# Causal attention and relu-squared MLP: six pairs scaled after the product with v, and two word conversions that may run on GpSimd

## Chip, cores, metric

One core of a Trainium2 chip runs the whole program. The metric is the device time of one execution in microseconds, lower is better.

## What is computed

q, k and v are float32 of shape (4 batches, 12 heads, 448 rows, 64 columns); w_in (768 x 2048) and w_out (2048 x 768) come as float64 words.

```python
scores = scale * q @ k.T            # causal mask, scale = 1/sqrt(64)
attn = exp(scores - max)            # masked
attn = attn / (sum(attn) + 1e-9)
x = (attn @ v)                      # laid out as 1792 tokens x 768
out = relu(x @ w_in)**2 @ w_out
```

## The kernel before

The program is written as a list of operations with ranks and dependencies (`plan.op`). A list scheduler, `Plan.emit`, gives each operation a place: at each step it takes the ready operation that can start first (ties by rank), and of the engines allowed for it (its "ways") the one that would end it first, with a small penalty of 0.5 us for ScalarE and 1.0 us for VectorE in the first part. Tiles from shared pools are taken and given back in that order, PSUM's eight banks too (kinds mm, sc, pt, av and others, each with a cap). The result is one fixed order for each engine's queue and for SyncE's DMA queue. Within a queue nothing overtakes: an instruction that waits holds up all that stand behind it.

Attention works on 24 pairs of heads. The first 12 (batches 0 and 1) are computed at the start, with two sets of buffers used in turn (`even`, names beginning with a, and `odd`, b). For one pair:

- `load_qk`, `load_v` (L349, L361): DMAs on SyncE; the first two pairs' q on ScalarE's queue.
- `transposed` (L367): VectorE turns k and q.
- `softmax` (L386): the scores of seven chunks of queries of 64 rows x 2 heads, chunk c against (c+1)*64 keys. The two heads of a chunk fill 128 partitions.
- `exponential`: VectorE adds the mask and takes the maximum (L399); ScalarE takes the exponential and its sum (L403) into the tiles p and sm.
- `inverse` (L470, L471): VectorE adds 1e-9 to the seven sums and inverts them.
- `normalise` (L412 on GpSimd, or L414 on VectorE): p of each of the seven chunks is multiplied in place by its inverse sums.
- `transposed_p` (L426): TensorE turns p in 16 blocks of 128 x 128, and ScalarE (L311) or VectorE (L434) copies four blocks at a time from PSUM to the tile pt.
- `times_v` (L446): v times pt gives x, transposed, in PSUM: 128 partitions (head and column) x 448 queries.
- For the first 12 pairs x is split into a float32r high part (ScalarE L311 from PSUM) and a low part (VectorE L314, PSUM minus high), both into x_t.

A next pair on the same buffers may write p only after the transposes of the pair before have read it.

Beside it the weights are brought in by `piece`: for each group gr (four in all) six pieces of w_in (128 x 512) and eight of w_out (128 x 384). A piece's float64 words are loaded (L587, three raw buffers), ScalarE converts the high word and the low word (two L311, words<-words), VectorE shifts, adds and joins them (L595, L314, L598), and `split` makes the high part on GpSimd (L324) or ScalarE and the low part on VectorE (L314) or GpSimd (L318). `h_unit` (L634 to L636) multiplies x of a half of the tokens by w_in; its two PSUM banks of kind mm let two columns of work be under way at once. Only the first group's w_in pieces are needed while the first pairs run.

After the first 12 pairs TensorE works on the MLP of the first two batches, group by group, with the other 12 pairs of attention put in between, and then on the second half of the tokens.

Of the kernel before, what the change touches and what calls it, by code (L numbers as in the profile page):

```python
# [9 lines left out]
F32 = mybir.dt.float32  # L10
F32R = mybir.dt.float32r
I32 = mybir.dt.int32
U32 = mybir.dt.uint32
I64 = mybir.dt.int64
AF = mybir.ActivationFunctionType
ALU = mybir.AluOpType

PE, ACT, DVE, POOL, DMA, DMA2 = range(6)
# [147 lines left out]
def t_dve(n, fast=False):  # L166
    return n / 1920 + 0.15 if fast else n / 960 + 0.15


def t_pool(n, two=False):  # L170
    return n * 0.0021 + 0.21 if two else n / 1200 + 0.22
# [9 lines left out]
def t_dma(count, size):  # L181
    return count * (0.0084 + size * 0.0000488) / 16
# [3 lines left out]
def kernel(  # L186
# [17 lines left out]
    nc = tc.nc  # L204
    B, H, S, D = q.shape
    DM = out.shape[1]
    DFF = w_in.shape[1]
    P = 128
    QC = P // 2
    NQ = S // QC  # L210
# [15 lines left out]
    PLACE = {6: (0, 0), 5: (1, 0), 0: (1, 6 * QC), 4: (2, 0), 1: (2, 5 * QC), 3: (3, 0), 2: (3, 4 * QC)}  # L226
# [10 lines left out]
    PCW = max(GF * P, CH)  # L237
    NRAW, NZ, NB, NR = 3, 3, 1, 6
    HWAY, OWAY, GWAY = slice(None), slice(1, 2), slice(0, 1)
    TURNS, LEAD = (0, 3, 2, 1), 15  # L240
    CB = NP // 2
    CBW = CB * P

# [15 lines left out]
    psum = ctx.enter_context(tc.tile_pool(name="psum", bufs=1, space=bass.MemoryType.PSUM))  # L259
    plan = Plan()  # L260

    def tiles(nm, n, shape, dtype, pool=const):
        return [pool.tile(shape, dtype, name=f"{nm}{i}") for i in range(n)]

    early = ExitStack()
    pool = early.enter_context(tc.tile_pool(name="early", bufs=1, side="right"))
    ident = pool.tile([P, 3 * QC], F32, name="ident")
# [3 lines left out]
    x_t = tiles("x", NA, [P, 2, S], F32R)  # L271
# [21 lines left out]
        nc.gpsimd.memset(t[KLAST:, NK - 1], 0.0)  # L293
    plan.pool("v", v_t)
    plan.pool("mx", tiles("mx", 8, [P, 1], F32))
    plan.pool("ps", tiles("ps", 8, [P, 512], F32, psum), mm=2, sc=4, pt=2, av=1, st=5, os=7)

    make_identity(nc, ident[:, :P])
    nc.vector.tensor_copy(ident[:, P:], ident[:, :QC])
# [1 line left out]
    for i in range(2):  # L301
        m = mask[i * QC:(i + 1) * QC, S - QC:]
        nc.gpsimd.affine_select(
            out=m, in_=m, pattern=[[-1, QC]], base=0,
# [5 lines left out]
    def on_act(n, dst, src, psum=False, func=AF.Copy, more=0, **kw):  # L310
        return (ACT, t_act(n, psum, more), lambda: nc.scalar.activation(dst(), src(), func, **kw))  # L311
# [8 lines left out]
    def two_sources(*args):  # L320
        return [on_dve(*args, 0.03) + SHARED, on_pool(*args)]
# [5 lines left out]
    def split(rank, n, hi, lo, src, reads, key, after=(), drop=(), take=None, ways=slice(None)):  # L327

        plan.op(rank, [copy_on_pool(n, hi, src), on_act(n, hi, src)],
                reads, [(key, 0)], after, drop=drop, take=take)  # L330
        plan.op(rank, two_sources(n, lo, src, lambda: hi().bitcast(F32), ALU.subtract)[ways],
                list(reads) + [(key, 0)], [(key, 1)], after, drop=drop)
# [4 lines left out]
    def attention(s, n, at):  # L337

        b, hp = divmod(n, NP)
# [68 lines left out]
        def normalise(c, keys, at):  # L408
            def operands():
                return probabilities(c), probabilities(c), s.sm[:, c:c + 1]  # L410
            plan.op(at, [
                (POOL, 0.00083 * CW[c] + 0.3, lambda: nc.gpsimd.tensor_scalar(  # L412
                    *operands(), 1.0, op0=ALU.mult, op1=ALU.mult)),
                (DVE, t_dve(CW[c], True) + 0.5, lambda: nc.vector.tensor_scalar(  # L414
                    *operands(), None, op0=ALU.mult)) + SHARED,
            ], keys, [(nm, "p", c)])

        def transposed_p(i, at):

            ps = Hold("ps", "pt")  # L420
            blocks = TURNED[4 * i:4 * i + 4]

            def go():
                for n, (c, kc) in enumerate(blocks):
                    o = QC * (PLACE[c][0] & 1)
                    nc.tensor.transpose(  # L426
                        ps.t[:, n * P:(n + 1) * P],
                        s.p[:, POFF[c] + kc * P:POFF[c] + (kc + 1) * P], ident[:, o:o + P])
            plan.op(at, [(PE, 4 * 0.109, go)], [(nm, "p", c) for c, _ in blocks], [ps],
                    take=ps, clear=[(nm, "pt", i)], lag=spare(1.6))  # L430
            t = s.pt[:, 4 * i * P:4 * (i + 1) * P]
            plan.op(at, [
                on_act(512, lambda: t, lambda: ps.t, True),
                (DVE, t_dve(512) + 0.05, lambda: nc.vector.tensor_copy(t, ps.t)),  # L434
            ], [ps], [(nm, "pt", i)], drop=[ps])
# [35 lines left out]
            nc.vector.reciprocal(s.sm, s.sm)  # L471
        keys = [(nm, "sm", c) for c in range(NQ)]
        plan.op(at, [(DVE, 0.4, inverse) + SHARED], [], keys)
        for c in range(NQ):
            normalise(c, keys, at)
        at += 2
        av = Hold("ps", "av")
        for i in range(len(TURNED) // 4):
            transposed_p(i, at)
        times_v(av, at + 1)  # L480
        at += 3
        if n < NA:
            x = x_t[n]
            plan.op(at, [on_act(S, lambda: x[:, 0], lambda: av.t[:, :S], True)],
                    [av], [(("x", n), 0)])
            plan.op(at, [on_dve(S, lambda: x[:, 1], lambda: av.t[:, :S],
                                lambda: x[:, 0].bitcast(F32), ALU.subtract)],
                    [av, (("x", n), 0)], [(("x", n), 1)], drop=[av])
        else:
            spill(n - NA, av, at)  # L490
# [69 lines left out]
    def piece(rank, kind, gr, a, ch, after):  # L560
        mark = len(plan.ops)
        if kind == "i":
            src = w_in[a * P:(a + 1) * P, gr * GF * P:(gr + 1) * GF * P]
            key = ("wi", a)
        else:
            f = gr * GF + a
            src = w_out[f * P:(f + 1) * P, ch * CH:(ch + 1) * CH]
            key = ("wo", a, ch)
        n = src.shape[1]
        raw, zt, bt = Hold("raw", "raw"), Hold("z", "z"), Hold("b", "b")  # L570

        def word(i):
            return raw.t.bitcast(I32).rearrange("p (c t) -> p c t", t=2)[:, :n, i]

        def z():
            return zt.t[:, :n]

        def zf():
            return z().bitcast(F32)

        def b():
            return bt.t[:, :n]

        def dst(i):
            return wi_t[:, i, a] if kind == "i" else late["wo"][:, i, a, ch * CH:(ch + 1) * CH]

        plan.op(rank - 12, [(DMA, 0.5, lambda: nc.sync.dma_start(out=raw.t[:, :n], in_=src), t_dma(P, 8 * n))],  # L587
                [], [raw], take=raw)

        plan.op(rank - 4, [on_act(n, zf, lambda: word(1).bitcast(F32), func=AF.Abs, scale=2.0 ** -112)],  # L590
                [raw], [zt], take=zt)

        plan.op(rank - 4, [on_act(n, b, lambda: word(0).bitcast(U32), scale=2.0 ** -29)],
                [raw], [bt], take=bt)
        plan.op(rank - 2, [(DVE, t_dve(n, True), lambda: nc.vector.tensor_scalar(  # L595
            z(), z(), 3, None, op0=ALU.logical_shift_left)) + SHARED], [], [zt])
        plan.op(rank - 2, [on_dve(n, z, z, b, ALU.add, 0.03) + SHARED], [bt], [zt], drop=[bt])
        plan.op(rank - 2, [(DVE, t_dve(n) + 0.03, lambda: nc.vector.scalar_tensor_tensor(  # L598
            out=z(), in0=word(1), scalar=-2 ** 31, in1=z(),
            op0=ALU.bitwise_and, op1=ALU.bitwise_or)) + SHARED], [raw], [zt], drop=[raw])  # L600
        split(rank, n, lambda: dst(0), lambda: dst(1), zf, [zt], key, after, [zt])
        if kind == "o":
            plan.op(rank, [(DMA, 0.5, lambda: nc.sync.dma_start(out=wo_dram[gr, a + GF * ch], in_=zf()), t_dma(P, 4 * CH))],
                    [zt], [("wod", gr, a, ch)], drop=[zt])
            if (a % 2, ch) != (0, 1) or gr == TURNS[-1]:
                plan.op(rank + 12, [(DMA, 0.5, lambda: nc.sync.dma_start(
                    out=wh_dram[gr, a + GF * ch],
                    in_=late["wo"][:, :, a, ch * CH:(ch + 1) * CH].bitcast(F32)), t_dma(2 * P, 4 * CH))],
                    [(key, i) for i in range(2)], [("whd", gr, a, ch)])
        if kind == "i" and gr > 0:  # L610
            plan.op(rank, [(DMA, 0.6, lambda: nc.sync.dma_start(
                out=wz_dram[gr, :, a // CB, :, a % CB].rearrange("f p n -> p f n"),
                in_=zf().rearrange("p (f n) -> p f n", n=P)), t_dma(P * GF, 4 * P))],
                [zt], [("wzd", gr, a)], drop=[zt])
        pieces.extend(plan.ops[mark:])
# [417 lines left out]
    PAIR = 8.6  # L1033
    H_US, O_US = 3 * t_mm(S), 3 * t_mm(CH)
    stack, middle = ExitStack(), ExitStack()
    odd = Buffers("b", stack.enter_context(tc.tile_pool(name="b", bufs=1)))
    for n in range(NA):
        attention((even, odd)[n % 2], n, n * PAIR)
    start = NA * PAIR + 4
# [36 lines left out]
    rank, begin = start, 10.0  # L1076
# [81 lines left out]
```

## Time and profile before

| What | us |
|---|---|
| Time, median of 3 runs (lowest to highest) | 615.87 (615.43 to 618.31) |
| Profiled execution: its own time | 616.22 |
| Profiled execution: span from first to last instruction | 614.5 |
| TensorE busy in the span | 589.3 |
| VectorE, ScalarE, GpSimd busy | 436.9, 356.7, 352.5 |

What lies outside the span of the profiled execution is 1.72 us. TensorE is counted busy while any of its matmuls is under way, also when one waits inside a group, so a busy engine may still work slower than it could.

### The profile page before, as it was taken

What the parts mean: (1) busy time and instruction counts of PE and PEld (TensorE: products, weight loads), DVE (VectorE), ACT (ScalarE), POOL (GpSimd) and SP (SyncE); (2) the same over time, 40 slices, a digit from 0 to 9 for tenths busy, and PEclk for the clock granted to TensorE, in tenths of its full rate; (3) what the DMA queues carried; (4) which work ended last, traced back from release to release, by engine and by line L of the source; (5) the groups of instructions that cost most, each with busy time, mean ns of one, the idle gap of its engine ahead of it and who ended that gap; (6) DMA issues with size and microseconds to landing.
All of it is one profiled execution on the core that took longest, in us unless ns stands there. A gap on an engine that the chain in (4) does not pass through costs nothing.

```text
span 614.5 us, 11390 instructions
## 1 busy us (share of the span) xinstructions
PE 589.3 (96%) x3714; PEld 511.0 (83%) x3714; DVE 436.9 (71%) x957; ACT 356.7 (58%) x878; POOL 352.5 (57%) x460
## 2 busy tenths in 40 slices
PE   3888999999999999999999999999999999999996
PEld 1555677789988988988998889989989999998995
DVE  4888776366786689785787326679994896399474
ACT  3787998657677845678555552247665534661220
POOL 2556575475589746788644764325865674478110
PEclk9899999999999999999999999999999999999999
DMA  9788856597888999998997477877958837963546
GB/s 140 159 199 146 175 99 132 106 308 243 249 222 256 293 264 220 275 265 277 245 279 249 163 209 220 266 219 194 228 103 198 224 71 161 221 105 95 149 76 106
DMA packets 203148, 120.01 MB, mean 195 GB/s; under 512 B 138960, under 2 KB 191056, under 8 KB 203088
## 3 DMA queue, kind: packets, MB, share of 16 engines
q1 hardware_dynamic: 181328, 108.01, 64.4%
q0 software_dynamic: 6912, 9.44, 10.2%
q10 hardware_dynamic: 14848, 1.84, 2.0%
q8 instruction: 29, 0.48, 0.3%
q14 instruction: 31, 0.25, 0.1%
HBM read 80.71 MB, written 38.54 MB: 194 GB/s over the span
## 4 chain that ended last, share of the span: by engine, by line
PE 81%; DVE 8%; DMA 5%; ACT 3%; issue 1%; POOL 1%; SPq 1%; DVEq 0%; ACTq 0%; POOLq 0%
PE ps L1010 7%; PE ps L634 7%; PE ps L1012 6%; PE ps L1011 6%; PE ps L636 6%; PE ps L635 6%; PE ps L426 6%; PE ps L446 6%; PE ps L386 5%; PE ps L937 5%; PE ps L939 5%; PE ps L938 5%; PE ps L815 4%; PE ps L811 4%; PE ps L813 4%; DVE g L314 2%
## 5 line engine op out<-in xcount | busy, mean ns | idle before, releaser
L412 POOL TENSOR_SCALAR ap<-ap,asm 128x128 f32<-128x128 f32 (+6 forms) x122 | 72.7, 615 | 52.3 <-DVE asm L471 41.6
L311 ACT ACTIVATE words<-words 128x384 f32<-128x384 f32 (+3 forms) x135 | 77.3, 596 | 32.9 <-DVE words L314 9.7
L399 DVE CUSTOM_DVE_ANT_0 ps<-ps,mask 128x448 f32<-128x448 f32 (+6 forms) x168 | 68.7, 444 | 28.2 <-PE ps L386 22.8
L1010 PE MATMUL ps<-wo,g 128*128 128x384 f32 x224 | 77.0, 344 | 0.0
L634 PE MATMUL ps<-x,wi 128*128 128x448 f32 x192 | 75.0, 391 | 0.6 <-ACT x L311 0.6
L1012 PE MATMUL ps<-wo,g 128*128 128x384 f32 x224 | 75.1, 335 | 0.0
L1011 PE MATMUL ps<-wo,g 128*128 128x384 f32 x224 | 75.0, 335 | 0.0
L636 PE MATMUL ps<-x,wi 128*128 128x448 f32 x192 | 70.9, 369 | 0.4 <-DVE wi L314 0.4
L635 PE MATMUL ps<-x,wi 128*128 128x448 f32 x192 | 70.7, 368 | 0.2 <-DVE x L314 0.2
L403 ACT ACTIVATE ap<-ps,mx 128x448 f32<-128x448 f32 (+6 forms) x126 | 58.7, 482 | 13.5 <-DVE mx L399 12.5
L937 PE MATMUL ps<-g,wi 128*128 128x448 f32 x162 | 59.5, 367 | 1.0 <-DVE sb L314 0.9
L311 ACT ACTIVATE r<-ps 128x448 f32<-128x448 f32 x59 | 32.1, 545 | 48.3 <-PE ps L815 15.8
L938 PE MATMUL ps<-g,wi 128*128 128x448 f32 x162 | 59.3, 366 | 0.0
L318 POOL TENSOR_TENSOR wi<-words,wi 128x384 fp32r<-128x384 f32 (+1 forms) x45 | 56.3, 1263 | 5.1 <-ACT wi L311 2.4
L939 PE MATMUL ps<-g,wi 128*128 128x448 f32 x162 | 59.2, 366 | 0.0
L324 POOL TENSOR_SCALAR wi<-words 128x384 fp32r<-128x384 f32 (+1 forms) x40 | 26.8, 672 | 47.4 <-DVE words L598 14.4
L811 PE MATMUL ps<-x,wi 128*128 128x448 f32 x141 | 51.8, 368 | 0.0
L813 PE MATMUL ps<-x,wi 128*128 128x448 f32 x141 | 51.7, 367 | 0.0
L815 PE MATMUL ps<-x,wi 128*128 128x448 f32 x141 | 51.7, 366 | 0.0
L314 DVE CUSTOM_DVE_ANT_0 words<-words 128x768 uint16<-128x768 uint16 (+1 forms) x56 | 45.7, 816 | 5.3 <-ACT words L311 1.9
L311 ACT ACTIVATE apt<-ps 128x512 f32<-128x512 f32 x70 | 38.4, 602 | 17.4 <-PE ps L426 17.4
L595 DVE TENSOR_SCALAR words<-words 128x384 int32<-128x384 int32 (+1 forms) x56 | 29.1, 521 | 21.5 <-ACT words L311 21.1
(138 smaller groups left out, 1476.1 us busy)
## 6 DMA issues: line engine op xcount, KB each, us to landing
words<-in_moe_w_in_dram SPq DMA_DIRECT2D x24, 512.0 KB, 5.3
words<-in_moe_w_out_dram SPq DMA_DIRECT2D x32, 384.0 KB, 4.2
wo_split<-wo SPq DMA_DIRECT2D x26, 384.0 KB, 4.8
wi<-wo_split SPq DMA_DIRECT2D x24, 384.0 KB, 4.5
wo_whole<-words SPq DMA_DIRECT2D x32, 192.0 KB, 4.0
wi_split<-wi SPq DMA_DIRECT2D x24, 256.0 KB, 4.0
v<-in_v_dram SPq DMA_DIRECT2D x24, 192.0 KB, 4.2
wi_whole<-words SPq DMA_DIRECT2D x18, 256.0 KB, 4.3
```

What stands on the lines that cost most here:

```text
L311: return (ACT, t_act(n, psum, more), lambda: nc.scalar.activation(dst(), src(), func, **kw))
L634: nc.tensor.matmul(o, w[:, 0], x[:, 0], start=c == 0, stop=False)
L635: nc.tensor.matmul(o, w[:, 0], x[:, 1], start=False, stop=False)
L636: nc.tensor.matmul(o, w[:, 1], x[:, 0], start=False, stop=c == NP - 1)
L811: nc.tensor.matmul(o, w.t[:, 0, c], x[:, 0], start=begin and c == 0, stop=False, skip_group_check=True)
L813: nc.tensor.matmul(o, w.t[:, 0, c], x[:, 1], start=False, stop=False, skip_group_check=True)
L937: nc.tensor.matmul(o, w.t[:, 0, d], g.t[:, 0], start=start, stop=False, skip_group_check=True)
L938: nc.tensor.matmul(o, w.t[:, 0, d], g.t[:, 1], start=False, stop=False, skip_group_check=True)
L939: nc.tensor.matmul(o, w.t[:, 1, d], g.t[:, 0], start=False, stop=stop, skip_group_check=True)
L1010: nc.tensor.matmul(res(), g[:, 0], w[:, 0], start=f == 0, stop=False)
L1011: nc.tensor.matmul(res(), g[:, 0], w[:, 1], start=False, stop=False)
L1012: nc.tensor.matmul(res(), g[:, 1], w[:, 0], start=False, stop=f == GF - 1)
```

## The change

For the first six pairs (n below 6, batch 0) p is left as the exponentials. `spread` takes the place of `normalise`: the inverse sums are laid on a stacked identity (VectorE or GpSimd, 128 x 448 elements), seven float32 matmuls of 64 columns with a 128 x 128 matrix of ones and zeros (`heads`) bring each query's factor to all partitions of its head, and the result is copied from PSUM to a tile xs (ScalarE or VectorE). After `times_v`, VectorE multiplies x in PSUM by xs into xs, and `split` makes the high part (GpSimd or ScalarE) and the low part (VectorE or GpSimd) from it. For the first group's pieces (gr 0) both word conversions get GpSimd as a second way. Some constants are set up on GpSimd at the start, and PSUM gets one more kind, rb, with a cap of one.

```diff
+    LATER = 6
-    TURNS, LEAD = (0, 3, 2, 1), 15
+    TURNS, LEAD, WORDS = (0, 3, 2, 1), 15, 0
@@
-    plan.pool("ps", tiles("ps", 8, [P, 512], F32, psum), mm=2, sc=4, pt=2, av=1, st=5, os=7)
+    plan.pool("ps", tiles("ps", 8, [P, 512], F32, psum), mm=2, sc=4, pt=2, av=1, rb=1, st=5, os=7)
@@
+        def spread(keys, at):
+            i = n % 2
+            rb = scaled[i].rearrange("p (c i) -> p c i", i=QC)
+            ps = Hold("ps", "rb")
+            plan.op(at, two_sources(S, lambda: rb, lambda: stacked[:, None, :].to_broadcast([P, NQ, QC]),
+                                    lambda: s.sm[:, :, None].to_broadcast([P, NQ, QC]), ALU.mult), keys, [("scaled", i)])
+            def go():
+                for c in range(NQ):
+                    cols = slice(c * QC, (c + 1) * QC)
+                    nc.tensor.matmul(ps.t[:, cols], heads[PLACE[c][0] & 1], scaled[i][:, cols],
+                                     start=True, stop=True, skip_group_check=True)
+            plan.op(at, [(PE, 0.8, go)], [("scaled", i)], [ps], take=ps)
+            xs = Hold("r", "xs")
+            plan.op(at, [on_act(S, lambda: xs.t, lambda: ps.t[:, :S], True),
+                         (DVE, t_dve(S) + 0.05, lambda: nc.vector.tensor_copy(xs.t, ps.t[:, :S]))],
+                    [ps], [xs], take=xs, drop=[ps])
+            return xs
@@
-        for c in range(NQ):
-            normalise(c, keys, at)
+        late_scale = n < LATER
+        if late_scale:
+            factors = spread(keys, at + 1)
+        else:
+            for c in range(NQ):
+                normalise(c, keys, at)
@@
+        if late_scale:
+            x, xs = x_t[n], factors
+            plan.op(at, [(DVE, t_dve(S) + 0.05, lambda: nc.vector.tensor_tensor(
+                out=xs.t, in0=av.t[:, :S], in1=xs.t, op=ALU.mult))], [av], [xs], drop=[av])
+            split(at, S, lambda: x[:, 0], lambda: x[:, 1], lambda: xs.t, [xs], ("x", n), drop=[xs])
+            return
@@
+        def early_pool(dst, src, scale):
+            return [] if gr > WORDS else [(POOL, t_pool(n), lambda: nc.gpsimd.tensor_scalar(
+                dst(), src(), scale, 1.0, op0=ALU.mult, op1=ALU.mult))]
@@
-        plan.op(rank - 4, [on_act(n, zf, lambda: word(1).bitcast(F32), func=AF.Abs, scale=2.0 ** -112)],
+        plan.op(rank - 4, [on_act(n, zf, lambda: word(1).bitcast(F32), func=AF.Abs, scale=2.0 ** -112)] + early_pool(
+            zf, lambda: word(1).bitcast(F32), 2.0 ** -112),
@@
-        plan.op(rank - 4, [on_act(n, b, lambda: word(0).bitcast(U32), scale=2.0 ** -29)],
+        plan.op(rank - 4, [on_act(n, b, lambda: word(0).bitcast(U32), scale=2.0 ** -29)] + early_pool(
+            b, lambda: word(0).bitcast(U32), 2.0 ** -29),
@@
+    stacked, heads = pool.tile([P, QC], F32, name="stacked"), tiles("heads", 2, [P, P], F32, pool)
+    nc.gpsimd.tensor_tensor(out=stacked, in0=ident[:, :QC], in1=ident[:, QC:P], op=ALU.add)
+    for h in range(2):
+        nc.gpsimd.memset(heads[h], 0.0)
+        for j in range(2):
+            nc.gpsimd.memset(heads[h][(j ^ h) * QC:((j ^ h) + 1) * QC, j * QC:(j + 1) * QC], 1.0)
```

## Rows read from the trace of the kernel before

**Rows 1.** The page's part 1: busy us, share of the span, instructions
```profile
PE 589.3 (96%) x3714; PEld 511.0 (83%) x3714; DVE 436.9 (71%) x957; ACT 356.7 (58%) x878; POOL 352.5 (57%) x460
```

**Rows 2.** Busy time by stage: us, per engine (instructions), granted clock, DMA share, GB/s
```profile
core 0: us, PE busy (x) PEld busy (x) DVE busy (x) ACT busy (x) POOL busy (x), PEclk, DMA share, GB/s
7.00:20.00 13.00, 8.74 (x80) 5.67 (x82) 9.01 (x35) 7.79 (x28) 3.20 (x7) 1.00 0.94 168
20.00:60.00 40.00, 34.71 (x306) 22.76 (x296) 34.16 (x110) 30.95 (x93) 22.72 (x41) 0.96 0.82 168
60.00:66.00 6.00, 4.82 (x30) 3.92 (x30) 2.56 (x7) 5.64 (x19) 2.70 (x3) 0.72 0.99 212
66.00:73.00 7.00, 6.73 (x60) 4.76 (x62) 6.64 (x23) 6.42 (x23) 5.36 (x9) 1.00 0.79 164
73.00:117.00 44.00, 44.00 (x384) 32.65 (x378) 30.04 (x107) 36.44 (x111) 22.89 (x41) 1.00 0.52 98
```

**Rows 3.** TensorE's timeline, 0 to 75 us: start, us, what, count, [idle before <-releaser]
```profile
13.42 3.09 PE L386 MATMUL ps<-bkt,bqt 64*64 64x448 f32 x28 [3.23 <-DVE asm L470]
...
19.46 0.99 PE L386 MATMUL ps<-akt,aqt 64*64 64x448 f32 x12 [1.03 <-ACT bp L403]
...
24.15 1.52 PE L426 MATMUL ps<-ident,bp 128*128 128x128 f32 x4 [0.77 <-POOL bp L412]
...
30.37 1.75 PE L386 MATMUL ps<-bkt,bqt 64*64 64x448 f32 x28
...
36.41 0.66 PE L426 MATMUL ps<-ident,ap 128*128 128x128 f32 x4 [0.77 <-ACT apt L311]
...
45.49 2.80 PE L386 MATMUL ps<-bkt,bqt 64*64 64x448 f32 x28 [1.02 <-ACT bpt L311]
...
61.18 1.94 PE L426 MATMUL ps<-ident,bp 128*128 128x128 f32 x8 [2.55 <-ACT ap L403]
...
66.26 1.95 PE L446 MATMUL ps<-bpt,v 128*64 128x448 f32 x16
```

**Rows 4.** ScalarE's timeline, the same columns
```profile
32.20 1.27 ACT L311 ACTIVATE words<-words 128x512 f32<-128x512 f32 x2 [1.07 <-DMA words<-in_moe_w_in_dram]
...
44.28 0.68 ACT L311 ACTIVATE words<-words 128x512 f32<-128x512 f32 x1 [1.71 <-DMA words<-in_moe_w_in_dram]
...
59.20 1.22 ACT L311 ACTIVATE words<-words 128x512 f32<-128x512 f32 x2 [3.09 <-DMA words<-in_moe_w_in_dram]
```

**Rows 5.** Granted clock around the two slow places, columns as in Rows 2
```profile
26.00:28.00 2.00, 1.62 (x5) 1.38 (x5) 1.74 (x7) 1.98 (x9) 1.47 (x2) 0.61 0.67 110
28.00:30.00 2.00, 2.00 (x11) 1.88 (x10) 0.93 (x4) 0.60 (x1) 1.16 (x4) 0.54 0.66 121
...
60.00:62.00 2.00, 0.82 (x4) 0.78 (x5) 0.64 (x3) 2.00 (x8) 1.92 (x3) 0.64 0.92 110
62.00:64.00 2.00, 2.00 (x9) 1.81 (x8) 1.48 (x3) 2.00 (x5) 0.78 (x1) 0.50 0.83 312
```

**Rows 6.** GpSimd's timeline, 0 to 75 us
```profile
13.86 3.20 POOL L412 TENSOR_SCALAR ap<-ap,asm 128x64 f32<-128x64 f32 x7 [10.85 <-DVE asm L471]
...
45.16 1.27 POOL L318 TENSOR_TENSOR wi<-words,wi 128x512 fp32r<-128x512 f32 x1
...
55.27 4.32 POOL L412 TENSOR_SCALAR bp<-bp,bsm 128x64 f32<-128x64 f32 x7
```

**Rows 7.** Chain that ended last, in order of time: start, us, what
```profile
105.66 1.31 PE ps L426 x12
```

**Rows 8.** Groups by form, 0 to 70 us: busy us, mean ns
```profile
L314 DVE TENSOR_TENSOR x<-ps,x 128x448 fp32r<-128x448 f32 x6 | 3.7, 614 | 1.9 <-ACT x L311 1.9
...
L324 POOL TENSOR_SCALAR wi<-words 128x512 fp32r<-128x512 f32 x5 | 3.1, 617 | 14.9 <-DVE bsm L470 8.9 <-DVE words L598 6.1
```

**Rows 9.** VectorE's timeline, 0 to 75 us
```profile
34.32 0.14 DVE L399 DVE_READ_ACCUMULATOR2_ANT mx<- 128x1 f32 x1
...
45.38 1.33 DVE L595 TENSOR_SCALAR words<-words 128x512 int32<-128x512 int32 x1
```

More of the change, by code (lines that the diff above doesn't have):

```diff
@@ L1035 @@
     stack, middle = ExitStack(), ExitStack()
-    odd = Buffers("b", stack.enter_context(tc.tile_pool(name="b", bufs=1)))
+    pool = stack.enter_context(tc.tile_pool(name="b", bufs=1))
+    odd, scaled = Buffers("b", pool), tiles("scaled", 2, [P, S], F32, pool)
+    stacked, heads = pool.tile([P, QC], F32, name="stacked"), tiles("heads", 2, [P, P], F32, pool)
[4 more added lines that the diff above has]
+            nc.gpsimd.memset(heads[h][(j ^ h) * QC:((j ^ h) + 1) * QC, j * QC:(j + 1) * QC], 1.0)
     for n in range(NA):
```

## The prediction, on record before the change was timed

> **What bounds the kernel now.** I read the page's busy times first: TensorE is busy 589.3 of 614.5 us [rows 1]. A change to softmax can then win only where TensorE stands, or works below its pace, and it loses wherever it gives TensorE work that finds no gap. The second view, busy time by stage, says where the 25.2 us of idle time lie. From 7 to 73 us TensorE stands for 4.26 + 5.29 + 1.18 + 0.27 = 11.0 us; before 7 us it waits for the first loads; from 73 to 117 us it stands for nothing [rows 2]. So the six pairs that the change touches run in the one long stage in which TensorE is not the bound: the sixth pair's product with v starts at 66.26 us [rows 3]. If x of the sixth pair comes d us earlier, the full stretch behind it starts d earlier, and, since TensorE is the bound from there on, the end comes d earlier too.
>
> Which wait ends last in that stage is told by TensorE's timeline: 3.23 us before the second pair's scores and 1.03 before the third's, 0.77 us for normalised p, 0.77 and 1.02 us for ScalarE's copies out of PSUM, and 2.55 us at 58.6 us, the largest in the middle [rows 3]. The first two belong to the loading of q and k, which nothing here makes faster (the DMA engines are at 0.94 from 7 to 20 us [rows 2]). Behind the later ones ScalarE's timeline shows the same cause three times: its queue stood 1.07, 1.71 and 3.09 us at a conversion of weight words whose load had not landed [rows 4], and the copies and exponentials stood behind it. Last, the granted clock: it is at 0.61 and 0.54 from 26 to 30 us and at 0.64 and 0.50 from 60 to 64 us, each time after TensorE had worked little or stood, so there part of the work ran at 1.2 GHz [rows 5].
>
> No engine has much room: from 20 to 60 us VectorE is busy 34.16 of 40 us (85%), ScalarE 30.95 (77%), GpSimd 22.72 (57%), DMA at 0.82 [rows 2]. A gain there meets VectorE soon.
>
> **The change part by part.**
>
> Normalising goes. It is seven instructions a pair on GpSimd, 3.20 us when alone and 4.32 us when disturbed [rows 6], between the last exponential and the last transpose, and the next pair on the same buffers waits for those transposes. On TensorE's path this shows as 0.77 us at 24.15. The half clock from 26 to 30 us follows that slow stretch; TensorE is busy 1.62 + 2.00 us in those 4 us [rows 5], so some 1.7 us would be won with full clock there. Ends: 0.8 (the wait alone) and 2.5. I take 1.8, since most, but not all, of the idleness ahead of the clock's fall was that wait.
>
> Words may go to GpSimd. Two conversions for each of the six w_in pieces, 12 in all. No row shows GpSimd doing them; the nearest is its copy of 128 x 512 at 617 ns, and the far bound its two-source operation of that width at 1.27 us [rows 6, 8]. That is 7.4 to 15.2 us for GpSimd; I take 0.7 each, 8.4 us, against about 6 x 3.4 = 20 us of normalising that it loses. What matters is that a wait for a load then blocks GpSimd and not ScalarE. At 58.6 us TensorE gets back up to 2.55 us, and up to half of the 2.82 us that it worked at the low clock from 60 to 64, 1.4 us, so 0 to 3.95; I take 3.0, as the 3.09 us wait of ScalarE covers the whole of it [rows 3 to 5]. At 45.5 us it is 1.02 us of standing and the stretch of the scores there (2.80 us where the same 28 took 1.75 at 30.37 [rows 3]), so 0 to 2.07; I take 1.2. At 36.41 us, behind the 1.07 us wait, 0 to 0.77; I take 0.7, the shortest wait being most surely gone. The eight w_out pieces of the first group lie mostly after 73 us, where GpSimd and ScalarE have room (22.9 and 36.4 of 44 us [rows 2]): nothing; without that room 16 x 0.6 us of GpSimd.
>
> Queued behind a waiting conversion on GpSimd stand the stacked product, the high and low parts of x and the normalising of the seventh and later pairs; TensorE waits for each of them in turn, for the first at the seven new matmuls. That is the first rival.
>
> New matmuls. Seven float32 products of 64 columns with 128 x 128 weights for a pair; float32 products stand in this trace as two instructions each (28 for the 14 scores), so 14. The nearest rows are the transposes, with the same weights and 128 columns: 12 in 1.31 us, 109 ns each [rows 7]. So 14 x 0.109 = 1.5 us is the upper end, and half, 0.76 us, the lower if only columns count. I take 1.1, since some of the pitch is weights: 6.6 us for six pairs, between 4.6 and 9.2. The stage has 11.0 us of idle time, and after the gains above some 5 remain; with that and the gaps inside groups I let two thirds of the new work find room: 2.2 us on the path (ends 0 and 6.6).
>
> New steps on x. Before: ScalarE's high part from PSUM and VectorE's low part, 614 ns [rows 8]. After: VectorE's multiplication, one source in PSUM (the same form, 614 ns), then high and low from SBUF; ahead of it the stacked product (1.2 us on GpSimd by the two-source row, 0.6 on VectorE) and a copy from PSUM. If low parts and stacked products go to GpSimd, VectorE is left with what it had; if both go to VectorE, it has 6 x 2 x 0.61 = 7.4 us more. GpSimd, relieved of 20 us and charged with 8.4 + 6 x (1.2 + 0.6 + 1.2) = 26 us, is still under the 85% of VectorE. The scheduler's penalty is on VectorE, so I take no more VectorE work. Each x comes later by about one instruction, 0.6 us, which counts once, at the sixth: but the transposes of that pair come over 3 us earlier, and hide it.
>
> Set-up constants: seven small GpSimd instructions at the start. GpSimd stands 10.85 us until 13.86 [rows 6]: nothing; without that, below 2 us. The number of DMAs is the same; their order on SyncE's queue may differ.
>
> A rule that speaks against the change: VectorE and GpSimd get in each other's way. VectorE's shift of a 512-wide piece took 0.42 us alone at 34.32 and 1.33 us when it started at 45.38, just after GpSimd's 1.27 us operation [rows 6, 9]. The Trainium skill (SBUF — State Buffer, "Who interferes with whom") says that the two share one pair of ports, and that a VectorE instruction with both inputs in SBUF collides with a GpSimd one that reads SBUF; the trace agrees for that shift, which has one input, and does not separate the two-input case. By that rule the low part would become such an instruction, which it was not while it read PSUM, and six of them could each lose up to a GpSimd operation. In the rows' terms that is 6 x 0.91 = 5.5 us of VectorE time at most; it is part of the third rival.
>
> Sum: 1.8 + 3.0 + 1.2 + 0.7 = 6.7 us gained, 2.2 given back: 4.5 us. The profiled execution took 616.22 us, which gives 611.7; the median is 0.35 below that execution. I say 611.5.
>
> **The rivals.**
>
> 1. The wait only changes its engine. Loads land when they land (DMA at 0.82 to 0.99 in this stage [rows 2]); GpSimd stands at the words, and x parts and the new matmuls stand behind it. Then 3.0 + 1.2 + 0.7 are not won: 1.8 - 2.2 = 0.4 lost, 616.3. For it: three loads were late already, and a shorter stage asks for them sooner. Against: GpSimd's work is needed less at once than ScalarE's.
>
> 2. The loop of two buffers is what counts. Scores of the fourth pair start at 30.37, of the sixth at 45.49 [rows 3]: 15.1 us for two pairs, of which over 3 us is normalising. If each of about two and a half such turns gets 3 us shorter, 7.5 to 8 us, plus part of the stall at 58.6: some 9.5 us, 606.5. Against: VectorE at 85% allows about 5 of 40 us and then is the bound.
>
> 3. Slower: VectorE is made the bound. From 20 to 60 us it has 5.8 us left [rows 2]. Low parts and stacked products on it are 7.4 us; six collisions with GpSimd like the one at 45.38 us, 1.33 - 0.42 = 0.91 us each [rows 9], are 5.5 us, of which I count a third, 1.8. 7.4 + 1.8 - 5.8 = 3.4 us longer in place of a gain, with the new matmuls' 2.2 us on top: 616.2 + 5.6 = 622. It decides where VectorE takes more than half of the new two-source work. For it: the scheduler takes whichever engine ends first, and GpSimd needs twice the time. Against: its penalty on VectorE.
>
> 4. The change does not do what it says: conversions stay on ScalarE because GpSimd is booked with stacked products and x parts. Then the three stalls stay; 616.3 as in 1.
>
> **How the numbers follow.** Forecast (609 to 612.8): 0.41. Rival 1: 0.19, rival 4: 0.07, rival 2: 0.17, rival 3: 0.16. A measurement of this kernel tells about 0.5%, 3.1 us, from no change: faster means below 612.8. Forecast and rival 2 are faster, 0.58; rivals 1 and 4 are the same, 0.26; rival 3 slower, 0.16. The range: 605 takes in most of rival 2; 620 all of 1 and 4 and the mild cases of 3. Of the forecast alone it would be 608.5 to 613.5.
>
> **What would show it.** Right: no wait of ScalarE for words before 70 us, and GpSimd doing the conversions; no 2.55 us gap near 58; the sixth pair's product with v some 4 us before 66.26; the new matmuls at 1.1 us a pair; full clock in the second place at least. Wrong: TensorE waiting for GpSimd's stacked product or x parts (rival 1); VectorE above 95% in 20 to 60 us (rival 3); that product at 58 us or sooner (rival 2). A gain up to 73 us that the later stages give back would break the step from x to the end.

## The result

The changed kernel takes 623.6 us (median of 6, 622.18 to 625.71) against 616.36 (median of 6, 615.43 to 618.31) of the kernel before on the same chip: 1.0106 times, 95% interval 1.0084 to 1.0129, about 6.5 us slower by that ratio (the two medians lie 7.2 us apart). The forecast was 611.5, the range 605 to 620.

The page's busy times come first, then busy time by stage, in the columns of [rows 2].

```profile
PE 597.6 (96%) x3798; PEld 518.8 (83%) x3798; DVE 440.5 (71%) x952; ACT 352.2 (57%) x866; POOL 363.4 (58%) x460
```

```profile
7.00:20.00 13.00, 11.10 (x90) 7.80 (x92) 8.19 (x34) 8.14 (x26) 2.27 (x3) 1.00 0.91 166
20.00:60.00 40.00, 39.87 (x386) 29.78 (x382) 33.55 (x107) 29.90 (x98) 23.50 (x27) 1.00 0.86 167
60.00:66.00 6.00, 4.52 (x50) 2.54 (x49) 5.17 (x21) 3.74 (x14) 4.61 (x8) 1.00 0.79 148
66.00:73.00 7.00, 6.87 (x46) 4.94 (x50) 6.66 (x15) 3.83 (x13) 6.50 (x11) 0.76 0.62 122
73.00:117.00 44.00, 43.72 (x372) 32.58 (x365) 32.19 (x107) 36.02 (x108) 24.62 (x40) 1.00 0.54 119
```

The span is 622.7 us, so TensorE stands 25.1 us in all, as it did before (25.2), and is busy 8.3 us more. From 20 to 60 us it now stands 0.13 us in place of 5.29 [rows 2]. VectorE is busy 33.55 us there, 84%, as before.

TensorE's timeline, in the columns of [rows 3]:

```profile
17.52 1.77 PE L430 MATMUL ps<-scaled,heads 128*128 128x64 f32 x14
...
26.87 1.77 PE L430 MATMUL ps<-scaled,heads 128*128 128x64 f32 x14
28.48 1.16 PE L447 MATMUL ps<-ident,ap 128*128 128x128 f32 x8
...
60.19 1.95 PE L467 MATMUL ps<-bpt,v 128*64 128x448 f32 x16
...
64.11 0.33 PE L447 MATMUL ps<-ident,ap 128*128 128x128 f32 x1 [0.29 <-POOL ap L413]
65.56 1.18 PE L447 MATMUL ps<-ident,ap 128*128 128x128 f32 x3 [1.12 <-POOL ap L413]
...
73.40 1.95 PE L467 MATMUL ps<-apt,v 128*64 128x448 f32 x16
```

The seven new matmuls (14 instructions, L430) take their place in the queue for 28.48 - 26.87 = 1.61 us (1.51 to 1.71 in the six pairs). The sixth pair's product with v starts at 60.19 us, 6.07 us sooner than in [rows 3]. The seventh's starts at 73.40, where it started at 74.44 before: the gain is nearly gone by then, in stops for GpSimd's normalising (L413) and a stretch at a lower clock (0.76 from 66 to 73 us). Part of the 6.07 us is order alone: between the two products TensorE now does 28 scores and 4 transposes more, and 3 products with w_in fewer, than before, some 1.6 us of work that before stood ahead of the sixth product.

The last matmul with w_out for the first half of the tokens parts the program in two. The rows below are of the kernel before and of the changed one: duration shortest/median/longest, then first and last start.

```profile
L1012 PE MATMUL ps<-wo,g x224: 333/334/347, 131.3 to 397.9; 128*128 128x384 f32 x112
```

```profile
L1049 PE MATMUL ps<-wo,g x224: 333/334/445, 126.9 to 398.9; 128*128 128x384 f32 x112
```

The last start is 397.9 before and 398.9 after: up to there the change costs 1.0 us in these two executions. From there to the end of the span it is 614.5 - 397.9 = 216.6 us before and 622.7 - 398.9 = 223.8 after: 7.2 us more in a half that the change does not touch. The next rows say for whom TensorE waited after 120 us (us in total, times, longest), first in the kernel before, then in the changed one.

```profile
PE ps L937 <- DVE sb L314: 0.9, 1, 0.9
```

```profile
PE ps L974 <- DVE sa L315: 2.2, 2, 1.8
PE ps L974 <- DVE sb L315: 2.1, 2, 1.9
PE ps L975 <- DVE g L315: 1.6, 1, 1.6
PE ps L1049 <- POOL g L319: 1.5, 1, 1.5
PE ps L974 <- DVE f L315: 0.7, 1, 0.7
PE ps L848 <- ACT r L312: 0.6, 1, 0.6
```

Five of the six lie in the second half, and four of these name VectorE. The 1.5 us for GpSimd's g is at 212 us, in the first half. The other five make 7.2 us, 6.3 more than the 0.9 us before, so they hold most of what the second half has lost.

### The profile page after: what moved, and what is told of

It reads as the page before. It is cut to its first block, busy times and chain, and to the rows that moved or that the text cites. A ratio compares the mean times of both kernels' runs of the same rounds, so it can differ in the third digit from the quotient of the medians.

```text
span 622.7 us, 11537 instructions
## 1 busy us (share of the span) xinstructions
PE 597.6 (96%) x3798; PEld 518.8 (83%) x3798; DVE 440.5 (71%) x952; ACT 352.2 (57%) x866; POOL 363.4 (58%) x460
## 4 chain that ended last, share of the span: by engine, by line
PE 85%; DVE 7%; POOL 4%; ACT 2%; issue 1%; DMA 1%; DVEq 0%; POOLq 0%; ACTq 0%
PE ps L467 7%; PE ps L447 7%; PE ps L671 7%; PE ps L673 6%; PE ps L672 6%; PE ps L1047 6%; PE ps L387 6%; PE ps L1049 6%; PE ps L1048 6%; PE ps L848 5%; PE ps L852 5%; PE ps L850 5%; PE ps L974 4%; PE ps L976 4%; PE ps L975 4%; DVE g L315 2%
## 5 line engine op out<-in xcount | busy, mean ns | idle before, releaser
L413 POOL TENSOR_SCALAR ap<-ap,asm 128x64 f32<-128x64 f32 (+6 forms) x100 | 65.1, 667 | 33.2 <-DVE asm L492 25.8
L312 ACT ACTIVATE words<-words 128x384 int32<-128x384 uint32 (+3 forms) x111 | 63.2, 593 | 29.5 <-DVE words L315 12.6
L319 POOL TENSOR_TENSOR wi<-words,wi 128x384 fp32r<-128x384 f32 (+1 forms) x49 | 63.1, 1349 | 9.3 <-ACT wi L312 8.0
L312 ACT ACTIVATE r<-ps 128x448 f32<-128x448 f32 x65 | 35.4, 546 | 52.6 <-PE ps L852 17.7
L404 ACT ACTIVATE ap<-ps,mx 128x448 f32<-128x448 f32 (+6 forms) x126 | 58.4, 480 | 11.1 <-DVE mx L400 10.4
L974 PE MATMUL ps<-g,wi 128*128 128x448 f32 x153 | 56.4, 369 | 5.0 <-DVE sa L315 2.2
L975 PE MATMUL ps<-g,wi 128*128 128x448 f32 x153 | 56.0, 366 | 1.6 <-DVE g L315 1.6
L976 PE MATMUL ps<-g,wi 128*128 128x448 f32 x153 | 55.9, 365 | 0.0
L312 ACT ACTIVATE r<-r 128x448 f32<-128x448 f32 x69 | 39.2, 576 | 10.3 <-DVE r L315 9.3
L315 DVE CUSTOM_DVE_ANT_0 words<-words 128x768 uint16<-128x768 uint16 (+1 forms) x56 | 39.9, 713 | 6.4 <-POOL words L619 1.6
```

The source lines that it names most:

```text
L974: nc.tensor.matmul(o, w.t[:, 0, d], g.t[:, 0], start=start, stop=False, skip_group_check=True)
L975: nc.tensor.matmul(o, w.t[:, 0, d], g.t[:, 1], start=False, stop=False, skip_group_check=True)
```

## The experiments

Kernels of one group ran on one chip and are compared with the kernel before there, in five rounds each. Ratios are to that kernel's time, with the 95% interval.

The first question is where the second half's 7 us come from. The scheduler places all operations in one pass, so when the first pairs take another time in its plan, it also draws the second half anew. The second half's 1131 operations (all from the preparation of x for the second half on) get another engine in 84 cases. To part the two, an order was written down from one kernel and kept in the other:

```diff
+ORDERED = [(operation, way), ...]   # the second half, in the order it was placed
...
             for o in ready:
+                if o in fixed and o is not late_ops[ORDERED[placed][0]]:
+                    continue
...
                     for i, w in enumerate(o.ways)
+                    if o not in fixed or i == ORDERED[placed][1]
```

**E1: the change, with the second half's order of before.**

> The changed kernel, whose operations of the second half of the tokens keep the order and the engines that they have in the kernel before. Theory A (in the second half the loss comes from the order that the scheduler draws anew when the first part's plan moves): the last matmul with w_out of the first half stays 1.0 us later than before, the stops of TensorE after 400 us go, the time is about 1 us above the kernel before, 617.4. Theory B (the second half is slow because of what the first half hands over: transfers or tiles that come at another time): the stops stay, 623 to 624.

1.0029 (1.001 to 1.0049), about 1.8 us. In the profiled execution the last w_out matmul starts at 397.6 us, and what follows takes 216.8 us, as in the kernel before. That execution took 616.18 us, 3.45 below the median of the twelve, so it does not say where the 1.8 us lie: with this order of the second half, the part after the last w_out matmul took from 216.4 us (E13) to 220.4 us (E11) in the profiled executions of the kernels below. A microsecond or two of theory B (the loss comes from what the first half hands over) is not excluded.

One stop stays in the first half, where E1 fixes no order, at 211 us:

```profile
PE ps L1124 <- POOL g L394: 1.7, 1, 1.7
```

All kernels here that scale six to eight pairs late have it, with 0.9 to 1.8 us; E15 has one of 1.2 us at 171 us for VectorE instead, and the kernel before, E2, E4, E7, E8 and E12 have none. So the part from 75 to 398 us, too, is paid for being drawn anew.

**E2: the kernel before, with the second half's order of the change.**

> The kernel before, whose second half has the order and the engines of the changed kernel; the first six pairs and the words are untouched. Theory A: the same 7 us of stops after 400 us appear without the change, 623 to 624. Theory B: 616.4, no stops.

1.0077 (1.0051 to 1.0103), about 4.8 us, and four of the changed kernel's five stops after 398 us, with nothing of the first pairs changed. The 1.6 us for g is not among them:

```profile
PE ps L1012 <- DVE sa L389: 2.3, 2, 1.8
PE ps L1012 <- DVE sb L389: 2.1, 2, 1.9
PE ps L1012 <- DVE f L389: 0.7, 1, 0.7
PE ps L886 <- ACT r L386: 0.6, 1, 0.6
```

E1's 1.8 us and E2's 4.8 us add up to the change's 6.5 within their intervals. So the order of the second half is the larger part, and theory A holds for it, though not with the full 7 us. How that order costs is seen in one of VectorE's groups by form after 398 us (count, busy us, mean ns), first in the kernel before, then in E2:

```profile
L314 DVE TENSOR_TENSOR r<-r,f 128x448 f32<-128x448 f32 x9 | 8.8, 976 | 0.0
```

```profile
L389 DVE TENSOR_TENSOR r<-r,f 128x448 f32<-128x448 f32 x8 | 15.4, 1924 | 0.1
```

The same operation of 128 x 448, both inputs in SBUF, takes 976 ns on the mean in one order and 1924 in the other; eight of them lose 7.6 us. VectorE's busy time after 398 us rises from 161.25 to 166.42 us. E2's trace shows what makes them long. Two places in it, VectorE's and GpSimd's timeline:

```profile
429.71 1.14 DVE L389 TENSOR_TENSOR r<-ps,r 128x448 f32<-128x448 f32 x2
429.29 1.38 POOL L393 TENSOR_TENSOR wi<-words,wi 128x384 fp32r<-128x384 f32 x1
...
551.97 4.03 DVE L389 TENSOR_TENSOR r<-r,f 128x448 f32<-128x448 f32 x1
552.15 1.42 POOL L399 TENSOR_SCALAR g<-r 128x448 fp32r<-128x448 f32 x2
553.22 2.29 POOL L393 TENSOR_TENSOR wi<-words,wi 128x384 fp32r<-128x384 f32 x2
```

At 429.71 us two operations with one input in PSUM (ps) keep their usual time beside GpSimd's work; at 551.97 us one with both inputs in SBUF does not end before GpSimd is through with four. So it goes with all of this form (f32, 128 x 448, two inputs) after 398 us in E2: 38 that read PSUM while GpSimd calculates take 0.63 us at most; 16 with both inputs in SBUF and GpSimd at rest take 0.61 to 0.63; 16 with both inputs in SBUF and GpSimd at work take 0.62 to 4.03, 1.43 on the mean. In the kernel before, the last kind has 20 members with 0.94 on the mean. The Trainium skill (SBUF — State Buffer, "Who interferes with whom") says that a VectorE instruction with two SBUF inputs contends with a GpSimd one that reads SBUF, and the trace agrees.

This is the collision that the prediction weighed for the first pairs; it struck in another place. The prediction measured it by a shift of one input, whose undisturbed row is this one of the kernel before:

```profile
34.32 0.42 DVE L595 TENSOR_SCALAR words<-words 128x512 int32<-128x512 int32 x1
```

That the slower operations are what makes TensorE stop in E2 is likely, since its stops name VectorE, but no run took the collisions out of that order.

**E7 and E8: the kernel before, with two other second halves.** These orders are what the scheduler draws when only the scaling, or only the words, are changed.

> The kernel before with another second half: the order that the scheduler draws when only the scaling is changed (67 of 1131 operations on another engine). If any redrawing costs, because the order before happened to have few collisions of VectorE and GpSimd: 2 to 6 us above the kernel before. If e2's order was one bad draw: within 1 us.

> The kernel before with a third second half: the order that the scheduler draws when only the words get their second way (59 of 1131 operations on another engine). If any redrawing costs: 2 to 6 us above the kernel before. If e2's order was one bad draw: within 1 us.

1.005 (1.0027 to 1.0074) and 1.0076 (1.0053 to 1.0099), 3 and 4.7 us. All three redrawn orders cost; the order of the kernel before is a good one that no redrawing met. The mechanism is not the same in each. In E8 VectorE's busy time after 398 us is 167.8 us, in E7 161.3, as before (161.25), and E7's longest stop is for ScalarE, at 404 us:

```profile
PE ps L886 <- ACT r L386: 2.3, 1, 2.3
```

**E3 and E4: the two edits apart, second half as before.**

```diff
-    TURNS, LEAD, WORDS = (0, 3, 2, 1), 15, 0       # E3: scaling alone
+    TURNS, LEAD, WORDS = (0, 3, 2, 1), 15, -1
-    LATER = 6                                      # E4: words alone
+    LATER = 0
```

> Only the scaling of x in place of p; words stay on ScalarE; the second half as in the kernel before. Theory A: the new matmuls cost 6 x 1.6 = 9.7 us of TensorE; waits for normalised p go, ScalarE's stops at the words stay (some 5 us of idle time of the stage): 2 to 5 us above the kernel before, 618 to 621. Rival C (the words do nothing, the shorter loop wins all of the idle time): as e1, about 617.

> Only the second way for the words of the first group; p is normalised as before; the second half as in the kernel before. Theory A: ScalarE's three stops (5.9 us) go, TensorE gets back 3 to 5 us: 611.5 to 613.5. Rival C: GpSimd, still busy with normalising, stands at the loads instead or is given few words: 615.5 to 617.5.

E3: 1.0043 (1.0027 to 1.0058), 2.7 us slower, as expected. E4: 1.002 (0.9999 to 1.0041), 1.2 us slower where 3 to 5 us of gain were expected. The words alone win nothing. Who waited for loads of words from 7 to 90 us in E4 (us in total, times, longest; the profiled execution took 622.48 us, the longest of its twelve):

```profile
POOL words L694 <- DMA words<-in_moe_w_in_dram: 7.9, 6, 2.2
...
POOL words L694 <- DMA words<-in_moe_w_out_dram: 2.5, 1, 2.5
...
ACT words L387 <- DMA words<-in_moe_w_in_dram: 6.1, 2, 3.4
```

The scheduler splits the conversions between the two engines. Now both stand at the loads, GpSimd for 10.4 us and ScalarE for 6.1, and behind GpSimd's waits stands the normalising: the sixth pair's product with v starts at 62.78 us, 3.5 sooner than before, the seventh's at 77.03, 2.6 later. That is rival 1, for this edit alone.

**E5 and E9: fewer new matmuls.** In E9 the chunks 0 and 2, 3 and 5, 4 and 6 share a matmul of 128 columns and 1 has its own. E5 paired 0 and 1, 2 and 3, 4 and 6, in which chunk 1 takes the factors of the wrong head; its times are those of the same work.

```diff
-                for c in range(NQ):
-                    cols = slice(c * QC, (c + 1) * QC)
-                    nc.tensor.matmul(ps.t[:, cols], heads[PLACE[c][0] & 1], scaled[i][:, cols], ...)
+                for c, step, many in ((0, 2, 2), (3, 2, 2), (4, 2, 2), (1, 1, 1)):
+                    nc.tensor.matmul(cut(ps.t, c, step, many), heads[PLACE[c][0] & 1], cut(scaled[i], c, step, many), ...)
```

> As e1 (the change, with the second half's order of the kernel before), but the factors of a pair are spread by four matmuls in place of seven: chunks with the same matrix are taken two at a time (128 columns). Same sums, same order of the queues. If each of the 14 instructions costs its place in the queue (115 ns, as a transpose of 128 columns does), 8 cost 0.9 us in place of 1.6, and TensorE, full from 20 to 60 us, ends 6 x 0.7 = 4 us sooner than in e1: ratio to the kernel before about 0.996. If columns alone cost, the 1.6 us stays and the ratio is e1's, 1.003. If TensorE is not what bounds the stage, the matmuls get shorter and the time stays.

> As e5, with the four matmuls over the pairs of chunks that do share a matrix (0 and 2, 3 and 5, 4 and 6, and 1 alone): the change with 0.9 us of TensorE a pair in place of 1.6 and the second half's order of the kernel before. Theory L (with the matmuls shorter the loads of words, q and k bound the first stage): as e5, ratio 1.001 to 1.004. Theory P (TensorE's work alone bounds it): 0.996 to 0.998.

E5: 1.0024 (1.0004 to 1.0045). E9: 1.0007 (0.9988 to 1.0026). In both the four take 0.9 to 1.0 us a pair, for 448 columns as before, so the count of instructions costs and not the columns. In E9's timeline:

```profile
55.33 1.10 PE L507 MATMUL ps<-scaled,heads 128*128 128x128 f32 x8
```

Of the 6 x (1.61 - 0.94) = 4.0 us that the four matmuls free, E9 shows 1.4 against E1 (1.0029 less 1.0007); the two intervals overlap, so part of the 4 us at most comes off the end.

**E6: the seven matmuls twice.**

```diff
-                for c in range(NQ):
+                for c in [*range(NQ), *range(NQ)]:
```

> As e1, with the seven matmuls of each pair issued twice (the second time over the same PSUM, same result). If TensorE bounds the stage from 20 us on, all 6 x 1.6 = 9.7 us show in the time: ratio about 1.018. If part of them still lies in gaps: 1.006 to 1.012. If the stage is bound by VectorE or by the loads: 1.003.

1.0181 (1.0155 to 1.0208): 9.4 us more than E1 for 9.7 us more of matmuls. From 20 to 60 us, in the columns of [rows 2]:

```profile
20.00:60.00 40.00, 40.00 (x382) 31.08 (x385) 26.80 (x81) 24.66 (x79) 18.16 (x21) 1.00 0.73 151
```

TensorE is full, VectorE at 67%. So upwards from seven matmuls each microsecond counts in full; downwards (E9) something else is met soon.

**E10, E11, E12: fewer rows loaded.** Of q and k of the pairs with n from 3 to 8 (the fourth to the ninth) only the first 64 of 448 rows are loaded, in as many transfers: E10 is E9 with that, E11 is E1, E12 the kernel before.

```diff
+                few = slice(0, 2 if 3 <= n < 9 else S // SQ)
-                    out=t[i:i + SQ].rearrange("p (b d) -> p b d", d=SQ),
+                    out=t[i:i + SQ].rearrange("p (b d) -> p b d", d=SQ)[:, few],
-                        "(b p) d -> p b d", p=SQ),
+                        "(b p) d -> p b d", p=SQ)[:, few],
```

> As e9, but of q and k of the pairs 3 to 8 only the first 64 of 448 rows are loaded (same number and order of transfers, the rest of those tiles keeps what an earlier pair left; attention of these pairs is therefore not the reference's). Theory L: the waits for words and k between 46 and 60 us go, 3 to 4 us below e9, ratio 0.995 to 0.998. Theory P: no change against e9.

> As e1 (seven matmuls, old second half), with the same lighter loads of the pairs 3 to 8 (same part left out). If TensorE, full from 20 to 60 us, bounds the stage by itself: as e1, 1.002 to 1.004. If the loads bound it there too: 3 us or more below e1.

> The kernel before with the same lighter loads (same part left out). If its three waits of ScalarE for words (5.9 us) come from transfers that share the DMA engines: they shrink and the time falls by 3 to 5 us, ratio 0.992 to 0.995. If they come from late issues on SyncE's queue: no change.

E10: 1.0002 (0.998 to 1.0023), as E9: theory L falls. E11: 1.0023 (0.9999 to 1.0046), as E1. E12: 0.9893 (0.9866 to 0.9919), 6.6 us faster. From 20 to 60 us in E12:

```profile
20.00:60.00 40.00, 36.75 (x325) 24.87 (x319) 35.63 (x116) 35.58 (x105) 24.40 (x43) 0.96 0.57 137
```

DMA is at 0.57 where it was at 0.82 [rows 2], and ScalarE's three waits for words [rows 4] are gone. So in the kernel before it is the sharing of the DMA engines that makes the words late. The 6.6 us are for all that the lighter loads change: two waits of VectorE for q, 1.0 us each at 29 and 51 us, are gone too, and the run does not part them. With seven matmuls (E11) the same relief is worth nothing: TensorE has already filled that idle time, 39.87 of 40 us. With four (E10) it is worth nothing either, and there the hand-over below stands behind it.

**E13, E14, E15: the hand-over.** In E9 TensorE still stands, for the most part at one place. Its timeline and two stretches of busy time:

```profile
56.37 1.95 PE L544 MATMUL ps<-bpt,v 128*64 128x448 f32 x16
...
63.72 2.18 PE L524 MATMUL ps<-ident,ap 128*128 128x128 f32 x5 [1.74 <-POOL ap L488]
...
73.00 1.95 PE L544 MATMUL ps<-apt,v 128*64 128x448 f32 x16
...
20.00:60.00 40.00, 38.78 (x381) 27.37 (x379) 33.89 (x110) 30.07 (x97) 25.82 (x30) 1.00 0.90 172
...
66.00:73.00 7.00, 6.28 (x44) 4.26 (x44) 4.87 (x11) 3.74 (x8) 7.00 (x11) 0.58 0.89 160
```

The first pair that is normalised as before, the seventh, comes 16.6 us after the sixth, and TensorE stops for its normalised p and falls to a clock of 0.58. In the changed kernel GpSimd's timeline shows what stands before that normalising:

```profile
61.01 1.17 POOL L619 TENSOR_SCALAR words<-words 128x512 int32<-128x512 uint32 x1 [1.62 <-DVE words L315]
...
62.96 0.56 POOL L325 TENSOR_SCALAR x<-r 128x448 fp32r<-128x448 f32 x1
63.74 0.32 POOL L413 TENSOR_SCALAR ap<-ap,asm 128x64 f32<-128x64 f32 x1 [0.21 <-issue]
64.02 1.13 POOL L319 TENSOR_TENSOR x<-r,x 128x448 fp32r<-128x448 f32 x1
65.13 3.33 POOL L413 TENSOR_SCALAR ap<-ap,asm 128x128 f32<-128x128 f32 x6
```

It is a word conversion, two high parts (one of a weight piece, not shown) and, after one of the seven, the sixth pair's low part; the inverse sums themselves come from VectorE behind the sixth pair's multiplication. To see whether it is the hand-over (theory H) or something about the seventh pair itself (theory K), E9 was run with 7, 8 and 12 pairs scaled late (LATER).

> As e9 (four matmuls, old second half), with seven pairs scaled late in place of six. Theory H (the gain up to the sixth pair is lost at the hand-over to the first pair that is normalised as before: its sums are inverted behind the sixth pair's new multiplication on VectorE, its normalising stands behind that pair's low part on GpSimd, TensorE waits 2.6 us and falls to 1.2 GHz for 4 us): the hand-over moves one pair later, where more matmuls with w_in are at hand to fill it; 1 to 3 us below e9, ratio 0.996 to 0.999. Theory K (something before the seventh pair, as its loads or its scores, holds it at 72 to 74 us): the seventh pair's product with v stays at 72 to 74 us, ratio as e9 or above.

> As e13 with eight pairs. Theory H: no stop of TensorE for normalised p before 80 us, none at 1.2 GHz after 60 us, seventh pair's product with v at 66 to 69 us; against that 2 x 0.9 us more matmuls: 2 to 3 us below e9, ratio 0.995 to 0.998. Theory K: 2 us above e9.

> As e13 with all twelve pairs of the first part: no hand-over at all, and 6 x 0.9 = 5.6 us more matmuls than e9, most of them where TensorE is full. Theory H: 4.6 us won, 5.6 spent: 0 to 2 us above e9. Theory K: 5 us above e9.

E13: 1.0005 (0.9986 to 1.0025). E14: 1.0064 (1.0038 to 1.009). E15: 1.0008 (0.9983 to 1.0032). TensorE's products with v around the hand-over, in E13, E14 and E15, with a stop where there is one:

```profile
61.93 1.95 PE L544 MATMUL ps<-apt,v 128*64 128x448 f32 x16
...
71.35 2.39 PE L524 MATMUL ps<-ident,bp 128*128 128x128 f32 x10 [0.45 <-POOL bp L488]
...
75.84 1.95 PE L544 MATMUL ps<-bpt,v 128*64 128x448 f32 x16
```

```profile
71.90 1.95 PE L544 MATMUL ps<-bpt,v 128*64 128x448 f32 x16
...
78.80 1.53 PE L524 MATMUL ps<-ident,ap 128*128 128x128 f32 x4 [0.84 <-POOL ap L488]
...
87.35 1.95 PE L544 MATMUL ps<-apt,v 128*64 128x448 f32 x16
```

```profile
61.80 1.95 PE L544 MATMUL ps<-apt,v 128*64 128x448 f32 x16
...
108.18 1.95 PE L544 MATMUL ps<-bpt,v 128*64 128x448 f32 x16
```

The gap moves with the hand-over: with seven pairs it lies between the seventh (61.93) and the eighth (75.84), with eight between the eighth (71.90) and the ninth (87.35), and with twelve there is none, the seventh pair comes at 61.80 and the twelfth at 108.18, where it was 111.57 in E9. Theory K falls. Of theory H's times one holds: E15 was to lie 0 to 2 us above E9 and lies 0.1 above, so its 6 x 0.94 = 5.6 us of further matmuls are won back, though not more. The two others fail: E13 was to be 1 to 3 us faster than E9 and is not faster by what can be measured, and E14 was to be 2 to 3 us faster and is 3.5 us slower. Moving the hand-over moves its stops: E14 stands for 2.8 us between 73 and 120 us, E9 for 3.1 between 60 and 73. E14's last w_out matmul starts 1.8 us after E9's, which two more pairs of matmuls (1.9 us) cover; the rest of the 3.5 us stays open.

## Why the prediction was wrong, step by step

**Where the idle time lies and what fills it** was right. The stop for words at 58.6 us, the waits at 24, 36 and 45 us and the half clock at both places are gone; the sixth pair comes 6.07 us sooner where some 4 were expected, 1.6 of them by order alone. Up to 120 us idle time fell from 18.8 to 10.9 us, and the clock's loss (one less the granted clock, times the stretch) from 3.4 us [rows 5] to 7 x 0.24 = 1.7, in a new place. That is 9.6 us regained, where the prediction's 6.7 us of gains and 4.4 us of hidden matmuls make 11.1.

**The new matmuls were mis-sized.** The value taken was 1.1 us a pair; measured 1.61, above even the upper end of 1.5 that the transposes gave, as the lower end (only columns count) is refuted: an instruction of 64 columns takes 115 ns, and E9's, mostly of 128 columns, take 0.94 / 8 = 117. Six pairs cost 9.7 us in place of 6.6. The Trainium skill (TensorE: Matmul & The Clock Gate, "LDWEIGHTS (loading the stationary operand)") puts the time in ns of a load of weights at their columns over 1.2, which is 107 ns for 128; the other operand's size is not in that formula. The 115 ns at 64 columns agree with that as a floor.

**That two thirds of them find room was the failed step of the first half.** The prediction looked for that room in the some 5 us of idle time that its gains leave of 11.0. But 4.26 of the 11.0 us lie before 20 us [rows 2], where only the first of the six pairs' matmuls stands (17.52 us). The other five pairs' lie between 26.87 and 60.19 us. There the kernel before has 5.29 us of idle time and 1.7 us of clock loss [rows 2, 5], 7.0 in all, and five times 1.61 is 8.1: they take all that the gains free. TensorE is at 39.87 of 40 us, and E6 shows that there they count in full. So the 9.6 us regained pay for 9.7 us of matmuls, and nothing is won. Up to 398 us the stop at 212 us is added: the trace loses 1.0 us, E1 1.8 us (0.6 to 3.0).

**"If x of the sixth pair comes d sooner, the end comes d sooner" did not hold** even inside the first half: 6.07 us at the sixth pair were 1.04 at the seventh. Of the 5.0 us between, 1.6 are order, as said above; the rest are 1.4 us of stops for normalised p and 1.7 us of clock, because the kernel goes back to normalising there. E13 to E15 place these stops at that hand-over. The prediction named GpSimd's queue ahead of the seventh pair's normalising, but gave it no price.

**From x to the end** the step failed outright: 4.7 us of the 6.5 are what E1 leaves for the second half's order, and E2 shows 4.8 by that order alone. The prediction took the later stages as given. It said of the scheduler only that DMA orders may differ, and it listed a gain given back in the later stages as what would break it, without a cause or a chance.

**The words** were credited with 4.9 us. Alone they win nothing (E4). Added to the scaling they win E3 minus E1, 0.9 us, which the two intervals do not tell from none.

**Rival 3** gave 622, near the time, by a mechanism that did not occur: VectorE is at 84% from 20 to 60 us, not above 95%, and the low parts and the stacked products of all six pairs went to GpSimd. Rival 1 is what E4 shows, for the words alone.

## What to carry to other kernels

Where one greedy pass orders a whole program, a change in its first part is a redrawing of all that follows: keep the later order fixed to measure the change itself, and take the spread of redrawn orders (here 3 to 5 us, all to the worse) into the range. Work given to the engine that bounds the program has to be set against the idle time of the very stretch in which it stands, after the gains have taken theirs. A speed-up of the first items of a pipeline is worth what is left of it one item past the boundary, so read the chain there too.

## What was not expected of the hardware

A float32 product of 64 columns with 128 x 128 weights costs 115 ns for each of its two instructions, as much as one of 128 columns: 1.61 us for 14 against 0.94 for 8 (E9). Lighter loads of q and k of six pairs (a seventh of the rows) took 6.6 us off the kernel before (E12) and nothing off the changed one (E10, E11). In E2 a VectorE operation with both inputs in SBUF took 0.61 us with GpSimd at rest and up to 4.03 us beside it; 38 with one input in PSUM took 0.63 us at most beside it.
